# A fused attention and FFN kernel: its fallback flag, branch hints, last store, lane order, first loads and masks are changed

## The chip, the core and the metric

The kernel runs on one core of one Trainium2 chip. The metric is the device time of one execution in microseconds. Five engines with queues of their own work side by side: TensorE (PE, with its weight loads shown as PEld), VectorE (DVE), ScalarE (ACT), GpSimd (POOL) and SyncE (SP), which issues nearly all DMAs here. Each engine runs its instructions in the order in which they were built and waits at semaphores for the others.

## The reference

```python
def _attn_ref(q, k, v, n_sink, window):            # (4, 8, 768, 64) each; 4 and 128
    scores = (1.0 / np.sqrt(D)) * np.matmul(q, k.transpose(0, 1, 3, 2))
    is_sink = pos[None, :] < int(n_sink)
    rel = pos[:, None] - pos[None, :]
    keep = is_sink | ((rel >= 0) & (rel < int(window)))
    scores = np.where(keep, scores, -1000000000.0)
    a = np.exp(scores - np.max(scores, axis=-1, keepdims=True))
    a = a / (np.sum(a, axis=-1, keepdims=True) + 1e-09)
    return np.matmul(a, v).astype(np.float32)

def _moe_ref(x, w_in, w_out):                      # (3072, 512), (512, 2048), (2048, 512)
    h = x @ w_in
    g = np.where(h >= 1, h, np.where(h <= -1, 0.0, (h + 1.0) ** 2 / 4.0))
    return (g @ w_out).astype(np.float32)

x = np.ascontiguousarray(_attn_ref(...).transpose(0, 2, 1, 3)).reshape(B * S, H * D)
```

## The kernel before

**Work and tiles.** Attention falls into 64 units: a batch, a head and half a sequence, which is three tiles of 128 queries. A unit's scores are three matmuls (260 columns: two blocks of 128 keys and 4 sink keys; the first tile of a sequence has 128), then DVE adds the mask and finds each row's peak, ACT takes the exponential, PE transposes the result, ACT copies it back and PE multiplies by the values. The first 16 units go as eight pairs of heads (`pair_scores`, L656; the exponential, L676; `early_transp`, L699, with its copies L705, L706 and L708 by ACT; `pair_r`, whose copy xn is L762; `pair_av`, L722), and the first four of these stand ahead of everything else in `first_pairs`. The other 48 are native units, whose scores are L444 and whose q_l, the low part of the queries, is made by POOL (L426).

The FFN goes by eight chunks of 384 rows of x. `split` makes x from xn in a high (ACT, L875) and a low part (DVE, L876), `stage1` multiplies by w_in (L835), and ACT and DVE make g (L842 to L847); `stage2` multiplies by w_out (L858), and ACT copies 128 rows of the output to SBUF (L869), from where SP stores them (L871). All FFN products are three matmuls of high and low parts. The weights come as 64-bit words in 16 blocks of 1 MB (`block`: one load by SP, L359; three DVE steps L361 to L365, a cast of the high part by ACT, L367, and the low part by DVE, L368).

**Masks.** m0, m1, m1n and m2 are added to the scores. DVE makes them at the start from iotas of POOL and from the two parameters (par_i, loaded by SP). That code, and memsets of the sink tiles behind them, lie ahead of the region in which the order is fixed by hand, and are ordered by the scheduler.

**Order.** `Plan` records every step with its engine, a guessed time, and what it reads and writes. `order` runs a list schedule over these guesses, and the steps are then issued in that order, which the region of `tc.manual_schedule()` keeps. PE has two lanes, A (attention) and B (FFN); `turn` picks between their heads, when both are ready, by the share of each lane's work that is done. The loads of SP are ordered by the due time of their readers, and one may go a set lead ahead of it.

**The end.** `checks` and `result` make a flag: whether the inputs were of the kind for which the fast path is right. The plan has them behind all chunks: DVE's checks, a PE transpose (L978), and three small DVE steps (L972 to L974) that write the tile other. Then every engine loads other (L1030) and branches (L1031) over a general computation of more than 10,000 instructions to the closing block (L1098).

## Time and profile before

| | us |
|---|---|
| median of 3 runs | 689.83 (688.82 to 690.71) |
| profiled execution | 689.68 |
| its span | 688.0 |
| TensorE's matmuls | 671.2 (98%) |
| DVE | 501.6 (73%) |
| ACT | 489.2 (71%) |
| POOL | 237.3 (34%) |

The span runs from the first to the last instruction of the profiled execution. TensorE is busy for nearly all of it, so what is to be read are the stretches in which it is not. TensorE's granted clock is 1.00, the upper of its two levels, in all stretches in which it has matmuls.

### The profile page before, as it was taken

To read this page: it belongs to the slowest core of one execution; us is meant where nothing else is said; L and a number is where in the kernel's file an instruction comes from. 1 tells how busy PE (TensorE), PEld (TensorE's weight loads), DVE (VectorE), ACT (ScalarE), POOL (GpSimd) and SP (SyncE) were. 2 spreads that over 40 slices of the span, in tenths; PEclk is the share of its full clock that TensorE was granted. 3 is DMA by queue.
4 is the path that set the end of the run, shared out by engine and by line. 5 is a ranking of instruction groups with operands and counts; after the bars stand their busy time and mean duration, and the time that the engine had idled before them with its cause. 6 is when DMAs were issued, how large, how long until landed. Compare 5 with 4: busy or idle time off the path is not lost.

```text
span 688.0 us, 11934 instructions
## 1 busy us (share of the span) xinstructions
PE 671.2 (98%) x3853; PEld 601.7 (87%) x3853; DVE 501.6 (73%) x1421; ACT 489.2 (71%) x1245; POOL 237.3 (34%) x421
## 2 busy tenths in 40 slices
PE   6899999999999999999999999999999999999995
PEld 5688888889999999999999999999999999999994
DVE  6998999787767688686786877787787776733221
ACT  6887877777668777887778777797777866544332
POOL 3000014444433445453543454354453444300000
PEclk9999999999999999999999999999999999999999
DMA  6946433231223433434434433434424221000001
GB/s 220 333 170 240 141 143 117 60 92 49 61 65 117 126 110 126 142 98 145 128 93 147 123 105 128 135 118 134 124 89 123 67 89 43 1 31 16 1 0 51
DMA packets 41086, 73.94 MB, mean 107 GB/s; under 512 B 4344, under 2 KB 25656, under 8 KB 41016
## 3 DMA queue, kind: packets, MB, share of 16 engines
q1 hardware_dynamic: 41016, 73.09, 33.4%
q8 instruction: 33, 0.54, 0.3%
q14 instruction: 37, 0.30, 0.1%
HBM read 66.78 MB, written 6.29 MB: 106 GB/s over the span
## 4 chain that ended last, share of the span: by engine, by line
PE 87%; DVE 7%; ACT 2%; DMA 1%; issue 1%; POOL 0%; SPq 0%; POOLq 0%; DVEq 0%
PE o_ps L858 36%; PE h_ps L835 36%; PE ps_a L587 5%; PE ps_a L444 5%; PE ps_a L525 2%; DMA w<-w_in 1%; PE ps_a L656 1%; DVE wi L368 1%; PE ps_a L722 1%; DVE gl L847 1%; DVE x L876 1%; DVE ends L363 1%; ACT p L452 1%; DVE ends L361 1%; DVE w L365 1%
## 5 line engine op out<-in xcount | busy, mean ns | idle before, releaser
L835 PE MATMUL h_ps<-x,wi 128*128 128x384 f32 x1536 | 311.8, 340 | 0.8 <-DVE x L876 0.6
L835 PEld LDWEIGHTS h_ps<-x,wi 128*128 128x128 f32 x1536 | 262.5, 188 | 10.4 <-issue 2.0
L858 PE MATMUL o_ps<-w,gh 128*128 128x512 f32 x768 | 243.4, 398 | 0.0
L858 PE MATMUL o_ps<-w,gl 128*128 128x512 f32 x384 | 151.0, 393 | 0.0
L858 PEld LDWEIGHTS o_ps<-w,gh 128*128 128x128 f32 x768 | 134.1, 188 | 15.8 <-issue 1.5
L844 DVE SCALAR_TENSOR_TENSOR g<-g,h_ps 128x384 f32<-128x384 f32 x128 | 70.4, 550 | 67.1 <-ACT g L843 66.3
L842 ACT ACTIVATE g<-h_ps,half 128x384 f32<-128x384 f32 x128 | 73.9, 577 | 54.1 <-PE h_ps L835 53.2
L847 DVE TENSOR_TENSOR gl<-g,gh 128x384 fp32r<-128x384 f32 x128 | 77.0, 602 | 29.4 <-ACT gh L846 28.8
L452 ACT ACTIVATE p<-p,peak 128x260 f32<-128x260 f32 (+1 forms) x144 | 71.6, 497 | 37.2 <-DVE peak L449 35.0
L846 ACT CAST gh<-g 128x384 fp32r<-128x384 f32 x128 | 65.3, 510 | 45.1 <-DVE g L844 43.9
L426 POOL TENSOR_TENSOR q_l<-r,q_h 128x384 fp32r<-128x384 f32 x48 | 50.6, 1053 | 116.9 <-ACT q_h L425 116.8
L858 PEld LDWEIGHTS o_ps<-w,gl 128*128 128x128 f32 x384 | 72.0, 188 | 16.9
L449 DVE CUSTOM_DVE_ANT_0 p<-ps_a,m 128x260 f32<-128x260 f32 (+1 forms) x144 | 57.7, 408 | 21.7 <-PE ps_a L444 21.4
L843 ACT ACTIVATE g<-g 128x384 f32<-128x384 f32 x128 | 67.2, 525 | 3.2
L471 DVE CUSTOM_DVE_ANT_0 p<-p,stat 128x128 f32<-128x128 f32 x128 | 60.1, 496 | 2.3
L546 POOL TENSOR_SCALAR_AFFINE_SELECT pt<-pt 128x384 fp32r<-128x384 f32 (+1 forms) x96 | 49.1, 514 | 23.7 <-ACT pt L534 12.6
L498 POOL TENSOR_TENSOR v_s<-r,v_s 128x256 fp32r<-128x256 f32 (+1 forms) x48 | 36.2, 754 | 60.1 <-ACT v_s L497 59.0
L551 POOL TENSOR_SCALAR_AFFINE_SELECT pt<-pt 128x384 fp32r<-128x384 f32 (+1 forms) x96 | 50.4, 545 | 0.2
L587 PEld LDWEIGHTS ps_a<-pt,v_s 128*128 128x128 f32 x304 | 42.5, 188 | 2.5 <-POOL v_s L498 0.2
L444 PE MATMUL ps_a<-k_s,q_l 128*128 128x260 f32 (+1 forms) x144 | 40.7, 283 | 1.3 <-POOL q_l L426 1.1
L587 PE MATMUL ps_a<-pt,v_s 128*128 128x256 f32 (+1 forms) x304 | 41.9, 275 | 0.0
L444 PE MATMUL ps_a<-k_s,q_h 128*128 128x260 f32 (+1 forms) x144 | 39.6, 275 | 0.0
(161 smaller groups left out, 851.6 us busy)
## 6 DMA issues: line engine op xcount, KB each, us to landing
r<-qk SPq DMA_DIRECT2D x48, 192.0 KB, 2.4
k_r<-qk SPq DMA_DIRECT2D x32, 262.0 KB, 2.8
w<-w_in SPq DMA_DIRECT2D x8, 1024.0 KB, 7.5
again<-w_in SPq DMA_DIRECT2D x16, 512.0 KB, 4.1
again<-w_out SPq DMA_DIRECT2D x16, 512.0 KB, 3.8
w<-w_out SPq DMA_DIRECT2D x6, 1024.0 KB, 8.5
out<-o SPq DMA_DIRECT2D x23, 256.0 KB, 2.4
r<-vx SPq DMA_DIRECT2D x32, 128.0 KB, 2.1
```

What stands on the lines that cost most here:

```text
L444: nc.tensor.matmul(ps()[:, lo:260], lhsT=q()[:, i * P:(i + 1) * P], rhs=k_s()[:, c0:c0 + 260 - lo], start=(j == 0), stop=(j == len(qs) - 1))
L449: op(DVE, 215 if lo else 350, lambda: nc.vector.tensor_tensor_reduce(out=p()[:, i, lo:260], in0=ps()[:, lo:260], in1=m, scale=-0.125, scal ...
L452: op(ACT, 400 if lo else 500, lambda: nc.scalar.activation(p()[:, i, lo:260], p()[:, i, lo:260], AF.Exp, bias=peak[:, n, i:i + 1], scale=-1.0,
L471: nc.vector.tensor_tensor_reduce(out=own, in0=own, in1=p()[:, k, 0:P], scale=r, scalar=0.0, op0=ALU.add, op1=ALU.add, accum_out=stat()[:, ...
L587: nc.tensor.matmul(z, lhsT=w, rhs=y, start=(n == 0), stop=(n == len(mms) - 1))
L835: nc.tensor.matmul(h_ps()[:, :T], lhsT=w_i[j][:, w, ct * P:(ct + 1) * P], rhs=x()[:, y, ct], start=(ct == 0 and n == 0), stop=(ct == NCT - ...
L842: op(ACT, 490, lambda: nc.scalar.activation(g(), h_ps()[:, :T], AF.Relu, bias=half, scale=0.5), r=[h_ps], w=[g])
L843: op(ACT, 440, lambda: nc.scalar.activation(g(), g(), AF.Square), w=[g])
L844: op(DVE, 470, lambda: nc.vector.scalar_tensor_tensor(g(), g(), 1.0, h_ps()[:, :T], op0=ALU.min, op1=ALU.max), r=[h_ps], w=[g])
L846: op(ACT, 420, lambda: nc.scalar.copy(gh(), g()), r=[g], w=[gh])
L847: op(DVE, 500, lambda: nc.vector.tensor_tensor(gl(), g(), gh().bitcast(F32), op=ALU.subtract), r=[g, gh], w=[gl])
L858: nc.tensor.matmul(ps(), lhsT=gg()[:, tt * P:(tt + 1) * P], rhs=w_o[j][:, w], start=(j == 0 and n == 0), stop=(j == NJ - 1 and n == 2))
```

## The change

Seven parts, in the order of the program:

- **Hints.** `mark_branch_hint_location` names the branch "other", likely taken, for all engines; the `If` bears that label and a preferred fall-through block. In the built program one BRANCH_PREFETCH_HINT is the first instruction of the main block on each engine.
- **Masks.** The region with the fixed order begins ahead of the masks. They are made directly as terms to be added, in 13 small DVE steps in place of some 26; parts of m1 and m2, which are needed later, are plan steps of DVE, ACT and POOL, and the tables of the native units are made by a POOL step, `setup`.
- **First queries.** The first pair's q_h goes by ACT's DMA queue, not SP's.
- **Third pair's loads.** They go to tiles of the rings q_l and k_r, and no longer wait for the first pair's tiles.
- **Slack and blocks.** `turn` takes the other lane's head when it has been ready for over 800 ns and the chosen one has not. The plan's link rate is 380 bytes per ns for the 1 MB blocks and 260 for other loads (before, 330 for all), and a block may always go 8000 ns ahead of its due time.
- **Flag.** `decide` (checks, transpose, result) stands in the middle of the last chunk.
- **Halves.** The last 128x512 of the output is copied as two halves: columns 0 to 255 by ACT and stored by ACT's queue, columns 256 to 511 by DVE and stored by SP.

```diff
@@ class Plan
+SLACK = 800
-                heapq.heappush(later[o.eng], (max(o.ready, o.due - (3000 if o.due < 25000 else 8000)) if o.eng == SP else o.ready, o.n, o))
+                heapq.heappush(later[o.eng], (max(o.ready, o.due - (8000 if o.due > 25000 or o.bytes == 1 << 20 else 3000)) if o.eng == SP else o.ready, o.n, o))
...
-                return a if done[ka] * LEAD * total[kb] <= done[kb] * total[ka] else b
+                x, y = (a, b) if done[ka] * LEAD * total[kb] <= done[kb] * total[ka] else (b, a)
+                return y if x.ready + SLACK > t >= y.ready + SLACK else x
...
-                link = max(link, free[e]) + o.bytes / 330.0
+                link = max(link, free[e]) + o.bytes / (380.0 if o.bytes == 1 << 20 else 260.0)
@@ masks, ahead of the plan's steps
+    region = ExitStack()
+    region.enter_context(tc.manual_schedule())
...
-    nc.vector.tensor_scalar(m2, rel, w_f, None, op0=ALU.is_lt)
...
-    for m in (m0, m1, m1n, m2):
-        nc.vector.tensor_scalar(m, m, -1.0, -NEG, op0=ALU.add, op1=ALU.mult)
...
+    nc.vector.tensor_scalar(skn, kpos, n_f, NEG, op0=ALU.is_ge, op1=ALU.mult)
+    nc.vector.scalar_tensor_tensor(ahead, rel[:, KB:260], w_f, ahead, op0=ALU.is_ge, op1=ALU.max)
+    nc.vector.tensor_tensor(m0, ahead, skn, op=ALU.mult)
+    nc.vector.scalar_tensor_tensor(m1n[:, 0:P], rel[:, 0:P], w_f, skn, op0=ALU.is_ge, op1=ALU.mult)
+    nc.vector.tensor_scalar(m1n[:, KB:260], ahead, NEG, None, op0=ALU.mult)
@@ def pair_load(m)
-        q_h, k_h = qh_ring.new(), ks_ring.new()
+        q_h, k_h = (ql_ring.new(), kr_ring.new()) if m == 2 else (qh_ring.new(), ks_ring.new())
...
-        op(SP, 420, lambda: nc.sync.dma_start(q_h().bitcast(F32), qkp[b, h // 2, :, 0:T]), w=[q_h], size=P * T * 4)
+        if m:
+            op(SP, 420, lambda: nc.sync.dma_start(q_h().bitcast(F32), qkp[b, h // 2, :, 0:T]), w=[q_h], size=P * T * 4)
+        else:
+            op(ACT, 420, lambda: nc.scalar.dma_start(q_h().bitcast(F32), qkp[b, h // 2, :, 0:T]), w=[q_h])
@@ def first_pairs()
+        op(DVE, 3600, lambda: None, w=["masks"])
+        op(DVE, 200, lambda: nc.vector.tensor_scalar(m2[:, 0:P], rel[:, 0:P], w_f, NEG, op0=ALU.is_ge, op1=ALU.mult),
+           r=["masks"], w=["m2"])
+        op(ACT, 200, lambda: nc.scalar.copy(m2[:, P:KB], skn[:, 0:NSINK]), r=["masks"], w=["m2a"])
+        op(ACT, 300, lambda: nc.scalar.copy(m2[:, KB:260], m1n[:, KB:260]), r=["masks"], w=["m2a"])
+        op(ACT, 300, lambda: nc.scalar.copy(m1[:, P:260], m2[:, P:260]), r=["m2a"], w=["m1a"])
...
+        op(POOL, 9000, setup, r=["m1"], w=["setup"])
...
@@ def stage1, last step
+        if plan.on and (row0, j) == (last, NJ - 3):
+            op(HOST, 1, lambda: tc.mark_branch_hint_location("other", "LikelyTaken", list(mybir.ALL_ENGINES)), r=[gl])
@@ def stage2, the last output
-            op(ACT, 500, lambda: nc.scalar.copy(at(), ps()), r=[ps] + [("xn", c, a) for c in range(NCT) for a in range(2)]
-               if end else [ps], w=[o])
-            op(SP, 420, lambda: nc.sync.dma_start(out[row0 + tt * P:row0 + (tt + 1) * P, :], at()), r=[o], size=1 << 18)
...
+            op(ACT, 320, lambda: nc.scalar.copy(o[:, h0], ps()[:, h0]), r=[ps] + x_k, w=["end0"])
+            op(DVE, 320, lambda: nc.vector.tensor_copy(o[:, h1], ps()[:, h1]), r=[ps] + x_k, w=["end1"])
+            op(ACT, 420, lambda: nc.scalar.dma_start(rows[:, h0], o[:, h0]), r=["end0"])
+            op(SP, 420, lambda: nc.sync.dma_start(rows[:, h1], o[:, h1]), r=["end1"], size=1 << 17)
@@ the chunks
         if c == len(chunks) - 1:
             ffn, attn = ffn + tail, []
+            ffn.insert(len(ffn) // 2, ("A", 0.1, decide))
...
-    plan.group = "A", len(chunks) + 1, 0.1
...
-    with tc.If(other_v > 0):
+    with tc.If(other_v > 0, preferred_fallthrough_block=True, label="other"):
```

What this makes of the order, at three places. Line numbers of the changed kernel are some lines off: L670 there is L676 before (the exponential), L702, L699 and L700 are L708, L705 and L706 (the copies of the transposed tiles), L756 is L762 (xn), L842 is L835 and L650 is L656.

ACT among the first four pairs, from the first 128-column exponential of the third pair, before (p and pt are halves of the exponentials' tiles of a pair, ps_a the PSUM bank in which PE left the transposes):

```order
L676 ACTIVATE p_203,stat_310<-p_203,peak_97 128x128
L762 COPY xn_163<-ps_a_298 128x384
L676 ACTIVATE p_203,stat_310<-p_203,peak_97 128x260 x2
L676 ACTIVATE p_205,stat_310<-p_205,peak_97 128x260
L708 COPY pt_240<-ps_a_327 128x384
L705 COPY pt_240<-ps_a_335 128x256
L706 COPY v_s_177<-ps_a_335 4x128
L708 COPY pt_229<-ps_a_342 128x384
```

The same place on ACT now:

```order
L670 ACTIVATE p_175,stat_328<-p_175,peak_83 128x128
L702 COPY pt_216<-ps_a_318 128x384
L699 COPY pt_216<-ps_a_323 128x256
L700 COPY v_s_144<-ps_a_323 4x128
L702 COPY pt_206<-ps_a_332 128x384
L699 COPY pt_206<-ps_a_339 128x256
L700 COPY v_s_145<-ps_a_339 4x128
L670 ACTIVATE p_175,stat_328<-p_175,peak_83 128x260 x2
L670 ACTIVATE p_179,stat_328<-p_179,peak_83 128x260
```

The six copies moved ahead of the three exponentials of 260 columns.

PE at the end of the first four pairs, from the transposes of the fourth pair's first unit, before (wi is the first w_in block):

```order
L699 MATMUL ps_a<-ident,pt 128x128 x5
L701 MATMUL ps_a<-ident,pt 4x128
L835 MATMUL h_ps<-x,wi_155 128x384 x3
L699 MATMUL ps_a<-ident,pt 128x128 x5
L701 MATMUL ps_a<-ident,pt 4x128
L742 MATMUL ps_a<-ident,stat 64x128 x6
L835 MATMUL h_ps<-x,wi_155 128x384 x3
L722 MATMUL ps_a<-pt,vq_176 64x128 x2
```

And now:

```order
L693 MATMUL ps_a<-ident,pt 128x128 x5
L695 MATMUL ps_a<-ident,pt 4x128
L693 MATMUL ps_a<-ident,pt 128x128 x5
L695 MATMUL ps_a<-ident,pt 4x128
L736 MATMUL ps_a<-ident,stat 64x128 x6
L716 MATMUL ps_a<-pt,vq_143 64x128 x2
L716 MATMUL ps_a<-pt,vq_143 64x256 x4
L716 MATMUL ps_a<-v_s,vq_143 64x128 x2
L650 MATMUL ps_a<-k_s,q_h 128x128 x2
L650 MATMUL ps_a<-k_s,q_h 128x260 x2
L842 MATMUL h_ps<-x,wi_124 128x384 x15
```

The two pieces of three FFN matmuls stand no longer among the pairs, but behind them and the next pair's scores.

ACT from the last outputs to the branch, with the semaphores that each row waits for, before (xn is the tile that the last output is put into):

```order
L869 COPY o<-o_ps 128x512 [waits DMAHW4_49,PE_49]
L869 COPY o<-o_ps 128x512 [waits DMAHW5_49,PE_49]
L869 COPY xn<-o_ps 128x512 [waits PE_49]
L1030 TENSOR_LOAD other [waits DVE_49]
L1031 COMPARE_AND_BRANCH
```

And now:

```order
L876 COPY o<-o_ps 128x512 [waits DMAHW4_49,PE_49]
L876 COPY o<-o_ps 128x512 [waits DMAHW5_49,PE_49]
L882 COPY xn<-o_ps 128x256 [waits DVE_49]
L884 DMA out<-xn 128x256 [waits Activation_49]
L1042 TENSOR_LOAD other [waits DVE_49]
L1043 COMPARE_AND_BRANCH
```

The last copy is half as wide and waits for DVE, whose copy of the other half stands ahead of it, and a store by ACT stands ahead of the load of the flag.

## Rows read from the trace of the kernel before

**Rows 1.** Busy time by stretch; columns as in the line above them.

```profile
core 0: us, PE busy (x) PEld busy (x) DVE busy (x) ACT busy (x) POOL busy (x), PEclk, DMA share, GB/s
4.86:34.34 29.48, 26.57 (x227) 19.09 (x227) 25.97 (x87) 24.38 (x83) 4.86 (x23) 1.00 0.86 299
...
112.70:190.00 77.30, 75.31 (x426) 68.17 (x426) 61.12 (x186) 57.33 (x158) 36.50 (x67) 1.00 0.23 63
190.00:681.03 491.03, 491.03 (x2741) 449.90 (x2739) 337.23 (x982) 346.31 (x857) 188.56 (x316) 1.00 0.30 92
681.03:688.00 6.97, 0.00 (x0) 0.00 (x0) 0.56 (x3) 0.51 (x1) 0.00 (x0) 0.76 0.35 125
```

**Rows 2.** Waits of PE: what waited for what; us in total, times, longest.

```profile
PE ps_a L699 <- ACT pt L708: 1.4, 2, 0.7
...
PE ps_a L699 <- ACT xn L762: 0.6, 2, 0.3
```

**Rows 3.** Timeline of the start: start, duration, engine, line, what; idle time before.

```profile
1.24 0.42 SPq L616 DMA_DIRECT2D k_s<-qkp  x1
...
1.71 0.42 SPq L618 DMA_DIRECT2D q_h<-qkp  x1
...
4.86 1.20 PE L656 MATMUL o_ps<-k_s,q_h 64*128 64x128 f32 x5 [4.86 <-DMA q_h<-qkp]
...
7.71 0.28 DVE L277 TENSOR_SCALAR m<-m 128x260 f32<-128x260 f32 x1
```

**Rows 4.** Chain of waits, the first weight block: start, duration, what.

```profile
10.32 7.08 DMA w<-w_in
```

**Rows 5.** Timeline of the pairs, and one row from behind them.

```profile
16.55 0.45 ACT L708 COPY pt<-ps_a 128x384 f32<-128x384 f32 x1
...
17.05 0.44 PE L699 MATMUL ps_a<-ident,pt 128*128 128x128 f32 x2 [0.71 <-ACT pt L708]
...
20.19 1.15 ACT L367 CAST wi<-w 128x1024 fp32r<-128x1024 f32 x1 [0.69 <-DVE w L365]
...
34.34 0.96 PE L835 MATMUL h_ps<-x,wi 128*128 128x384 f32 x4 [0.61 <-DVE x L876]
...
128.09 0.33 PE L444 MATMUL ps_a<-k_s,q_l 128*128 128x128 f32 x1 [0.63 <-POOL q_l L426]
```

**Rows 6.** Timeline of the end.

```profile
680.53 0.39 PE L858 MATMUL o_ps<-w,gl 128*128 128x512 f32 x1
...
680.76 0.27 PE L978 MATMUL ps_a<-ident,flag 128*1 128x128 f32 x1
680.96 0.59 ACT L869 COPY xn<-o_ps 128x512 f32<-128x512 f32 x1
...
681.57 0.33 SPq L871 DMA_DIRECT2D out<-xn  x1
```

**Rows 7.** Durations by line (ns: least, median, most), and issue to landing.

```profile
L592 DVE TENSOR_TENSOR xn<-ps_a,xn x48: 539/556/562, 129.0 to 600.7; 64x384 f32<-64x384 f32 x48
...
L705 ACT COPY pt<-ps_a x16: 351/368/383, 10.3 to 96.1; 128x256 f32<-128x256 f32 x16
...
out<-xn SPq DMA_DIRECT2D x1, 256.0 KB, 2.0
```

**Rows 8.** Line L1031, the branch: ns, then first and last start in us.

```profile
L1031 SPq EVENT_SEMAPHORE  x8: 17/17/17, 686.0 to 686.6; - x8
L1031 ACTq COMPARE_BRANCH  x1: 50/50/50, 682.5 to 682.5; - x1
L1031 POOLq COMPARE_BRANCH  x1: 45/45/45, 682.6 to 682.6; - x1
...
L1031 PEldq COMPARE_BRANCH  x1: 4306/4306/4306, 682.6 to 682.6; - x1
L1031 POOLq EVENT_SEMAPHORE  x1: 17/17/17, 682.8 to 682.8; - x1
...
L1031 ACTq EVENT_SEMAPHORE  x1: 17/17/17, 685.5 to 685.5; - x1
```

More of the change, by code (lines that the diff above doesn't have):

```diff
@@ L913, in attn_ffn, with checks, decide, result @@
     spn = [t().bitcast(F32).rearrange("p t a d -> p (t a d)")[:, 0:P] for t in sinks0]
-    for t in spn:
-        nc.vector.memset(t, 0.0)
     ends = dec.tile([P, 2, DM], I32, name="ends")
     spare = dec.tile([P, 2, 2 * DM], I32, name="spare")
-    with tc.issue_after(behind):
-        nc.gpsimd.memset(ends, 0)
     p0 = [p_ring.new() for _ in range(2)]
     pt0 = [pt_ring.new() for _ in range(2)]
+    flag = const.tile([P, CT], F32, name="flag")
+    other = const.tile([1, 1], I32, name="other")
+    def checks():
+        v, both = nc.vector, chk[1]
+        pk = peak.rearrange("p u i -> p (u i)")
+        v.tensor_tensor(pk, pk, pk, op=ALU.mult)
+        v.tensor_reduce(flag[:, 1:2], pk, axis=mybir.AxisListType.X, op=ALU.add)
+        v.tensor_scalar(flag[:, 0:1], flag[:, 1:2], LARGE2, None, op0=ALU.is_lt)
+        for value, bound, o in ((n_f, float(NSINK), ALU.is_le), (w_f, float(P), ALU.is_le), (w_f, 1.0, ALU.is_ge)):
+            v.scalar_tensor_tensor(flag[:, 0:1], value, bound, flag[:, 0:1], op0=o, op1=ALU.mult)
+        v.tensor_scalar(both, both, 0x38383838, None, op0=ALU.bitwise_and)
+        v.tensor_scalar(both, both, 0x38383838, None, op0=ALU.bitwise_xor)
+        v.tensor_scalar(both.bitcast(F32), both, 0.0, None, op0=ALU.is_equal)
+        v.tensor_reduce(flag[:, 1:2], both.bitcast(F32), axis=mybir.AxisListType.X, op=ALU.min)
+        v.tensor_tensor(flag[:, 0:1], flag[:, 0:1], flag[:, 1:2], op=ALU.mult)
+    def decide():
+        ps = bank_a.new()
+        def result():
+            nc.vector.tensor_reduce(flag[0:1, 1:2], ps()[0:1, :P], axis=mybir.AxisListType.X, op=ALU.min)
+            nc.vector.tensor_scalar(flag[0:1, 2:3], flag[0:1, 1:2], -1.0, 1.0, op0=ALU.mult, op1=ALU.add)
+            nc.vector.tensor_copy(other, flag[0:1, 2:3])
+        op(DVE, 4000, checks, w=["flag", "both"] + [("peak", n, i) for n in range(len(units)) for i in range(CT)])
+        op(PE, 110, lambda: nc.tensor.transpose(ps()[0:1, :P], flag[:, 0:1], ident), r=["flag"], w=[ps])
+        op(DVE, 700, result, r=[ps], w=["flag"])
     def run(steps, c):
```

120 lines of the change are left out of this document (48 added, 72 removed).

## The prediction

> **What bounds the kernel now.** I read the busy times by stretch first, then what TensorE waits for, then the timelines of the places where it stands still. TensorE's matmuls fill all of the 491.03 us from 190 us to the last matmul, 26.57 of the 29.48 us from the first matmul to 34.34 us, and 75.31 of the 77.30 us from 112.7 to 190 us [rows 1]. So TensorE is idle for 4.86 us before its first matmul, for 2.91 us in the stretch of the first four pairs, for 1.99 us after 112.7 us and for 6.97 us behind its last matmul, some 16.7 us in all. The change adds no matmul and takes none away: the most that it can give is this idle time, and the most that it can lose is new idle time. The profiled execution took 689.68 us against a span of 687.96 us (1.7 us lie around the span); the median of the runs is 689.83 us. Each term below is a difference of spans, so I take the sum from the median. About 0.3%, or 2.1 us, is what a measurement of this kernel can tell from no change; 687.8 us is the border to faster, 691.9 us that to slower.
>
> In the pairs stretch two waits are for the copy pt of L708, of up to 0.7 us each, and two for the copy xn of L762, 0.6 us together; both copies are ScalarE's [rows 2].
>
> **The change, part by part. First queries and masks.** SP issues its second load, k_s, at 1.24 us and its third, q_h, at 1.71 us; the first matmul needs both and starts at 4.86 us [rows 3]. In the changed kernel q_h is ScalarE's first instruction, but k_s is still SP's second. So only the 0.47 us by which q_h was later can go, and a part of it goes again because two loads now share the link: -0.4 us, between 0 and -0.6 (the 0.47 and what the fewer loads ahead of k_s might save). DVE's last mask step ends at 7.99 us, between the first reductions of the scores [rows 3]. Half of these steps are gone, so the first reductions and exponentials come sooner; I count nothing for that here, because TensorE does not wait for them until the pairs stretch, where it is a part of that term. If the new steps were slower than the old ones, the first transposes would be late by it.
>
> **The third pair's loads and the blocks.** The first weight block was issued at 10.32 us and landed 7.08 us later [rows 4], because it stood behind two loads whose buffers TensorE still read. With the third pair's loads in buffers of their own and the longer lead, it is SP's eighth load, and no load ahead of it waits. Seven issues of some 0.43 us put its issue near 4 us [rows 3], and the same 7.08 us its landing near 11 us. Alone this gives nothing: no matmul uses the block before the end of the pairs. It lets DVE, which waited for it, decode earlier, and that is a part of the next term.
>
> **The pairs stretch.** At 16.55 us ScalarE starts the copy L708, right behind three exponentials of the next pair, and TensorE starts the transposes behind it 0.50 us later, at 17.05, after 0.71 us of idle time [rows 5]. In the changed order the exponentials of 260 columns stand behind the copies, so the copy comes about 1 us sooner (two of about 0.5 us), more than the 0.71. The second wait for pt has a cast of a weight slice ahead of it on ScalarE, of 1.15 us, at 20.19 us [rows 5]. In the changed order the first such cast stands behind all exponentials of the fourth pair, and this second 0.71 us has no cause left either. Against these 1.42 us: the pieces of the first FFN product that filled TensorE among the fourth pair's transposes now all stand behind the pairs. That is no loss of work, but ScalarE has no less to do, and the idle time can come back at the first FFN pieces. Before, these waited 0.61 us for an x piece ahead of 34.34 us [rows 5]; with one weight cast fewer ahead of the last x cast I take 0.4 us of that. The waits for xn stay. Together -1.8 us, between 0 (each wait moves to ScalarE's next copy) and -2.9 (all idle time of the stretch). Beyond zero it could grow by one weight cast, 1.15 us, if TensorE comes to the FFN pieces that much ahead of x.
>
> **Slack.** After 112.7 us TensorE loses 1.99 us, of which 0.63 us in one wait for GpSimd's q_l [rows 1, 5]. The rule that takes a lane's head which has been ready for 800 ns over one that is only just ready changes the order there. The trace shows no such choice. I take -0.3 us, half of that one wait, between -2.0 (all of it) and +1.3 (two more such waits). Nothing is to be had from 190 us on, where TensorE has no idle time.
>
> **Flag, halves and hints: the tail.** The last matmul ends at 680.92 us, ScalarE's copy of 512 columns takes 0.59 us from 680.96, SP issues the store at 681.57 [rows 6], and it lands 2.0 us later [rows 7], near 683.6. That is not what ends the span. All engines take the branch over the general case near 682.6 us. SP's next instruction starts at 686.0 us and ScalarE's at 685.5; TensorE's branch itself lasts 4.31 us, to 686.9 [rows 8]. GpSimd, which takes the same branch, goes on within 0.2 us. From SP's 686.0 to the end of the span, at 688.0, are another 1.9 us of semaphores. So 3 to 4.3 us pass in which no engine does anything but get to the code behind the branch.
>
> With the flag made inside the last chunk its transpose costs TensorE 0.11 us inside the stream (before, it ended at 681.03 us, 0.11 us behind the last matmul [rows 6]). If the hint works, each engine's branch costs GpSimd's 0.2 us, and the stores set the end. DVE copies one half of 256 columns: 0.42 us, halfway between its 0.28 us for 260 columns in SBUF [rows 3] and its 0.556 us for 384 columns from PSUM [rows 7]. ScalarE's half takes the 0.368 us of its other copies of 256 columns [rows 7]. They do not run side by side: in the built order ScalarE's copy waits for DVE's. With 0.03 us at each of two hand-overs ScalarE's store is issued at 681.81 us, 0.24 us later than SP's was, and lands near 683.85. SP's wait for it and 1.83 of the 1.9 us of semaphores end at 685.68 in place of 687.96, 2.28 us sooner; less the 0.11 us of the transpose the term is about -2.15 us. Engines that load the flag first (0.8 us) and branch are all there before 683.85.
>
> If the hint does nothing, the branches only start sooner: ScalarE's near 683.0 us, since it now issues a store ahead of it, with its next instruction 3.0 us later at 686.0; TensorE's near 681.8, so that its 4.31 us end at 686.1 in place of 686.9. The end is then 0.9 us sooner.
>
> **The sum** with a hint that works: -0.4 - 1.8 - 0.3 - 2.15 = -4.65 us, and 689.83 - 4.65 = 685.2 us.
>
> **Rival A: the hint changes nothing.** For it: in the built order the hint is the first instruction of each engine's main block, some 680 us ahead of the branch, and whatever is fetched on it has the whole kernel in which to be displaced. Against it: a hint that names a branch could be kept until the engine comes to it. No row of before shows a hint, so both prices of the branch, 0.2 us and 3.0 to 4.31, stand as ends. 689.83 - 0.4 - 1.8 - 0.3 - 0.9 = 686.4 us.
>
> The Trainium skill's page "Runtime: NRT & Kernel Launch", section "Instruction fetch mechanics", speaks for this rival. It says that instructions are fetched ahead strictly in order, and that a taken branch to a place outside the window has to wait for a transfer of it. The trace agrees as far as a plain branch goes, by the 3 to 4.31 us on four engines [rows 8]; by that rule, which knows no hint, the sum would be this rival's. No run here shows yet what a hint does.
>
> **Rival B: the pairs stretch keeps its idle time.** ScalarE is busy for 24.38 of the 29.48 us there [rows 1], and what is taken from one of its copies may wait at the next. Against it: the two longest waits have named causes that are gone. 689.83 - 0.4 - 0.3 - 2.15 = 687.0 us, and with rival A 688.2.
>
> **Rival C: slower, by a hint that fetches at the wrong time.** The hint stands where the main block begins. If it makes an engine fetch the far code in place of what comes next, the engine pays the price of a fetch there and then. It is not hidden: SP's loads and TensorE's first matmul come behind it. TensorE's price is the longest, 4.31 us [rows 8]. One such stall, with the tail of rival A, gives 686.4 + 4.31 = 690.7 us, no change that can be measured; two, the second where displaced code is wanted again, give 695.0 us. So it decides from the second stall on. Against it: all that stands between is in order, which is how the engines ran 680 us without one.
>
> **How the numbers follow.** The forecast, 0.53, has its own range from 683.4 to 686.1. Rival A has 0.22, rival B 0.16 (687.0 to 688.2), rival C 0.06, and 0.03 are for a growth of the pairs stretch or of the one after 112.7 us. The forecast, rival A and two thirds of B lie below 687.8: faster 0.85. The rest of B and of the growth, with one stall of C: same 0.10. Slower 0.05. The range goes from 683.0 us (all idle time of the pairs, 0.6 us at the head and 1.2 of the 1.99 us, in the forecast's sum) to 688.1, where B meets A.
>
> **What would show it.** Right: behind the branch each engine goes on within 0.3 us, and the last store's landing is what SP waits for; no wait for pt above 0.3 us before the first FFN product; a first matmul at 4.4 to 4.5 us. Wrong: branches that still take 3 to 4 us (A); waits for pt, xn or x of together over 2 us in the pairs stretch (B); first loads that are microseconds later than now (C). A TensorE idle time of over 1 us between 190 us and the last matmul would break the sum wholly.

## The result

The changed kernel takes 694.31 us (median; 693.82 to 695.40), the kernel before 689.92 us beside it (688.82 to 690.71): a ratio of 1.0067, with a 95% interval of 1.0054 to 1.0081. It is slower, where 685.2 us and faster were forecast. The profiled span is 693.4 us against 687.96.

The end is shorter and the start is shorter; the loss lies where TensorE had no idle time at all. The busy time of the engines by stretch in the changed kernel (columns as in [rows 1]):

```profile
4.05:31.96 27.91, 26.25 (x226) 19.63 (x226) 24.67 (x84) 24.68 (x86) 4.69 (x23) 1.00 0.84 301
...
190.00:400.00 210.00, 207.08 (x1167) 188.21 (x1166) 160.19 (x473) 158.06 (x405) 91.69 (x157) 1.00 0.38 114
400.00:600.00 200.00, 197.10 (x1111) 178.93 (x1110) 154.29 (x450) 146.70 (x372) 92.37 (x149) 1.00 0.33 101
...
687.91:693.40 5.49, 0.00 (x0) 0.00 (x0) 0.42 (x1) 0.37 (x1) 0.00 (x0) 0.97 0.42 148
```

In [rows 1] the stretch from 190 us on was full. Here 5.8 us are idle in it (210 - 207.08 and 200 - 197.10). The stretch behind the last matmul is 5.49 us, where it was 6.97. What TensorE waits for in the changed kernel (us in total, times, longest), beside [rows 2]:

```profile
PE o_ps L650 <- DMA k_s<-qkp: 4.1, 1, 4.1
PE ps_a L516 <- DVE peak L440: 3.6, 8, 0.8
PE ps_a L578 <- POOL v_s L489: 1.8, 4, 0.8
PE ps_a L435 <- POOL q_l L417: 1.7, 4, 0.8
PE ps_a L693 <- ACT pt L702: 1.4, 1, 1.4
```

The first matmul starts 0.8 us sooner. The two waits for pt have become one of 1.4 us, and the waits for xn are gone. The native units now have 16 waits, where they had three: the transposes (L516) wait for DVE's peak, the values (L578) for GpSimd's v_s, the scores (L435) for GpSimd's q_l. Idle time tells only a part, for the same 3853 matmuls are busy for 674.7 us in place of 671.2. In a dense row a matmul starts before the one ahead of it has ended (0.11 us behind its start, of a run of 0.28, in the rows below), and a delay shows as idle time only as far as it is longer than this overlap. At the 23 places with idle time in the changed kernel the next matmul starts 12.4 us later, all told, than the same pair of shapes does in a dense row, of which 9.1 us are idle. So a wait takes, by this estimate, some 0.14 us more than its idle time shows. The waits that were added explain some 1.5 of the 3.5 us in this way; by the same estimate most of the rest are delays too short to leave a gap.

One such place, on TensorE, in the changed kernel:

```profile
365.43 0.28 PE L435 MATMUL ps_a<-k_s,q_h 128*128 128x260 f32 x1
365.54 0.29 PE L435 MATMUL ps_a<-k_s,q_l 128*128 128x260 f32 x1
...
365.91 0.28 PE L435 MATMUL ps_a<-k_s,q_h 128*128 128x260 f32 x1
366.03 0.28 PE L435 MATMUL ps_a<-k_s,q_l 128*128 128x260 f32 x1
366.15 1.21 PE L842 MATMUL h_ps<-x,wi 128*128 128x384 f32 x6
368.14 0.55 PE L516 MATMUL ps_a<-ident,p 128*128 128x128 f32 x3 [0.79 <-DVE peak L440]
```

and what GpSimd, DVE and ScalarE did for it:

```profile
364.22 1.02 POOL L417 TENSOR_TENSOR q_l<-r,q_h 128x384 fp32r<-128x384 f32 x1 [1.98 <-ACT q_h L416]
...
366.87 0.54 DVE L851 SCALAR_TENSOR_TENSOR g<-g,h_ps 128x384 f32<-128x384 f32 x1
367.33 0.41 DVE L380 TENSOR_TENSOR both<-both,top 128x256 int32<-128x256 int32 x1
367.67 0.41 DVE L440 CUSTOM_DVE_ANT_0 p<-ps_a,m 128x260 f32<-128x260 f32 x1
...
368.59 0.51 ACT L443 ACTIVATE p<-p,peak 128x260 f32<-128x260 f32 x1
```

The unit's three score tiles stand on end (a tile of q_h and q_l each from 365.43 to 366.03), q_l had been finished at 365.24, 0.30 us ahead of its first reader, and DVE reaches the tiles' peaks only at 367.67, behind its own queue. Score tiles that the next tile follows at once are 85 of 144 in the built order, where it was 2 before.

The transposes at 368.14 do not wait for their own operand. They belong to the unit before, for the exponentials of the tiles scored here begin only at 368.59. They wait for a place to write to: all of the native units' steps on TensorE share a ring of three PSUM banks.

```python
    bank_a = ring(ps_a, 3, "ps_a", [P, 512], F32)
```

The unit's three score tiles fill the ring, and its first bank is free again when DVE's peak step has read it, at 368.08 us (367.67 + 0.41). All eight of these waits are of this kind: the transposes of one unit begin 63 to 65 ns behind the end of the peak step on the first score tile of the next.

### The profile page after: what moved, and what is told of

The parts are those of the page before. It is cut to its first block, busy times and chain, and to the rows that moved or that the text cites. A ratio compares the mean times of both kernels' runs of the same rounds, so it can differ in the third digit from the quotient of the medians.

```text
span 693.4 us, 11948 instructions
## 1 busy us (share of the span) xinstructions
PE 674.7 (97%) x3853; PEld 602.1 (87%) x3853; DVE 506.2 (73%) x1410; ACT 488.4 (70%) x1248; POOL 240.2 (35%) x425
## 4 chain that ended last, share of the span: by engine, by line
PE 58%; DVE 17%; ACT 10%; issue 7%; POOL 5%; DMA 2%; SPq 0%; POOLq 0%; ACTq 0%; DVEq 0%
PE h_ps L842 24%; PE o_ps L867 24%; DVE p L462 3%; ACT p L443 3%; PE ps_a L578 3%; PE ps_a L435 2%; DVE gl L854 2%; DVE g L851 2%; POOL pt L537 1%; DVE x L890 1%; POOL q_l L417 1%; PE ps_a L516 1%; DVE k_s L414 1%; DMA r<-qk 1%; ACT gh L853 1%
## 5 line engine op out<-in xcount | busy, mean ns | idle before, releaser
L842 PE MATMUL h_ps<-x,wi 128*128 128x384 f32 x1536 | 309.4, 340 | 0.2 <-DVE x L890 0.2
L842 PEld LDWEIGHTS h_ps<-x,wi 128*128 128x128 f32 x1536 | 264.0, 188 | 11.2 <-issue 2.9
L867 PEld LDWEIGHTS o_ps<-w,gh 128*128 128x128 f32 x768 | 139.7, 188 | 18.8 <-issue 0.5
L854 DVE TENSOR_TENSOR gl<-g,gh 128x384 fp32r<-128x384 f32 x128 | 79.1, 618 | 32.6 <-ACT gh L853 31.5
L417 POOL TENSOR_TENSOR q_l<-r,q_h 128x384 fp32r<-128x384 f32 x48 | 52.6, 1096 | 73.5 <-ACT q_h L416 73.1
L440 DVE CUSTOM_DVE_ANT_0 p<-ps_a,m 128x260 f32<-128x260 f32 (+1 forms) x144 | 53.0, 408 | 11.0 <-PE ps_a L435 10.7
L489 POOL TENSOR_TENSOR v_s<-r,v_s 128x256 fp32r<-128x256 f32 (+1 forms) x48 | 34.0, 708 | 40.1 <-ACT v_s L488 36.2
L578 PEld LDWEIGHTS ps_a<-pt,v_s 128*128 128x128 f32 x304 | 41.7, 188 | 5.3 <-POOL v_s L489 3.9
L578 PE MATMUL ps_a<-pt,v_s 128*128 128x256 f32 (+1 forms) x304 | 42.6, 277 | 2.0 <-POOL v_s L489 1.8
L435 PE MATMUL ps_a<-k_s,q_l 128*128 128x260 f32 (+1 forms) x144 | 38.3, 288 | 1.8 <-POOL q_l L417 1.7
L526 DVE TENSOR_TENSOR pt<-ps_a,pt 128x384 fp32r<-128x384 f32 x48 | 26.6, 553 | 18.0 <-ACT pt L525 12.3
```

The lines of the kernel that those rows point to most:

```text
L417: op(POOL, 1020, lambda: nc.gpsimd.tensor_tensor(q_l(), q_r(), q_h().bitcast(F32), op=ALU.subtract), r=[q_r, q_h], w=[q_l])
L578: nc.tensor.matmul(z, lhsT=w, rhs=y, start=(n == 0), stop=(n == len(mms) - 1))
L842: nc.tensor.matmul(h_ps()[:, :T], lhsT=w_i[j][:, w, ct * P:(ct + 1) * P], rhs=x()[:, y, ct], start=(ct == 0 and n == 0), stop=(ct == NCT - ...
L854: op(DVE, 500, lambda: nc.vector.tensor_tensor(gl(), g(), gh().bitcast(F32), op=ALU.subtract), r=[g, gh], w=[gl])
L867: nc.tensor.matmul(ps(), lhsT=gg()[:, tt * P:(tt + 1) * P], rhs=w_o[j][:, w], start=(j == 0 and n == 0), stop=(j == NJ - 1 and n == 2))
```

## The experiments: which number of the plan

The parts of the change other than the plan's three numbers (slack rule, link rates, lead of the blocks) stay in the first three of these.

**no_slack**

```diff
-                return y if x.ready + SLACK > t >= y.ready + SLACK else x
+                return x
```

> The changed kernel with the slack rule taken out of the choice between the two lanes; the new link rates and block lead stay. Theory: the slack rule makes the order in which TensorE waits from 190 us on (2.92 us idle from 190 to 400 us and 2.90 us from 400 to 600 us, where before there was none). Then that idle time goes, and with it the 3.5 us by which the matmuls' busy time grew: near 686 us. Rival, the new link rates make the order: idle time of over 4 us stays between 190 and 600 us and the time stays within 1.5 us of 694.3.

692.45 us. Half of the theory holds at most: 0.34 us idle are left from 190 to 400 us, but 3.42 us from 400 to 600. The slack rule is not the only cause.

**old_rates**

```diff
-                link = max(link, free[e]) + o.bytes / (380.0 if o.bytes == 1 << 20 else 260.0)
+                link = max(link, free[e]) + o.bytes / 330.0
```

> The changed kernel with the plan's link rate back at 330 bytes per ns for all loads; slack rule and block lead stay. Theory slack: time stays near 694 us, TensorE's idle time from 190 to 600 us stays at 4 us or more. Rival rates: near 686 us and no idle time there.

697.47 us, slower than the change itself, with 7.4 us of TensorE's idle time from 190 to 600 us. The rival falls as well: with the slack rule in, the old rates do not mend the order.

**old_plan** has both edits and the old lead:

```diff
-... o.due - (8000 if o.due > 25000 or o.bytes == 1 << 20 else 3000) ...
+... o.due - (3000 if o.due < 25000 else 8000) ...
```

> The changed kernel with slack rule, link rates and block lead all as before; flag, hints, halves, masks, first queries and third pair's loads stay. TensorE's order is then that of before but for some 67 rows. If the order is the whole loss: no idle time of TensorE from 190 us to the last matmul, and 689.9 less the tail's 1.5 us and the start's 1 to 2.5 us, 686 to 687.5 us. If something else of the change (the hint at the program's start, the flag inside the last chunk, GpSimd's setup) costs the middle: 692 us or more.

681.46 us, a ratio of 0.9882 to the kernel before. The plan's numbers are the whole loss, 12.85 us, and what they hid is a gain of 8.6 us (690.04 beside it), nearly twice the 4.65 us that were forecast for everything together. TensorE's waits behind the first matmul are three:

```profile
PE ps_a L516 <- DVE p L460: 0.4, 1, 0.4
PE ps_a L693 <- ACT pt L702: 0.4, 1, 0.4
PE ps_a L716 <- ACT pt L702: 0.2, 1, 0.2
```

The place of the timeline above now reads so on TensorE: between the score tiles stand six matmuls of the FFN each.

```profile
366.64 0.28 PE L435 MATMUL ps_a<-k_s,q_h 128*128 128x260 f32 x1
366.76 0.28 PE L435 MATMUL ps_a<-k_s,q_l 128*128 128x260 f32 x1
366.88 1.20 PE L842 MATMUL h_ps<-x,wi 128*128 128x384 f32 x6
367.92 0.28 PE L435 MATMUL ps_a<-k_s,q_h 128*128 128x260 f32 x1
```

**lead_only** (no slack rule, old rates, the new lead of the blocks):

> The changed kernel without the slack rule and with the old link rate; only the longer lead of the weight blocks stays of the plan's numbers. Score tiles on end: 1 of 144, as with the old plan. Theory: that count decides, so 681 to 683 us, idle time of TensorE only where the blocks are decoded, ahead of 115 us. Rival: the lead of the blocks makes a part of the loss by itself: 685 us or more.

685.28 us: the rival. The lead alone costs 3.8 us. 3.25 us are idle between the first and the last matmul, where old_plan has 1.03, most of it between 112 and 190 us. The largest wait, on TensorE:

```profile
115.49 1.20 PE L842 MATMUL h_ps<-x,wi 128*128 128x384 f32 x6
118.25 0.55 PE L516 MATMUL ps_a<-ident,p 128*128 128x128 f32 x3 [1.56 <-DVE peak L440]
```

There DVE came to the peak at 117.91 us, behind work that stood ahead of it in its queue: attention's own steps and parts of x, none of them the decoding of a block. It is the same wait for a bank, 64 ns behind the end of that peak step. By which way the earlier blocks bring this about was not shown.

**rates_only** (no slack rule, old lead, the new rates):

> The changed kernel with the new link rates alone of the plan's three numbers (no slack rule, old block lead). Score tiles on end: 57. With the new lead as well it was 692.45 us, and the new lead alone cost 3.8 us over 681.46. If rates and lead add up: 688.6 us, with idle time of TensorE between 400 and 600 us as with both. If the rates are the whole of it: 692.5. If the rates do no harm without the lead: 681.5 to 682.5.

695.36 us, more than with the lead as well (692.45). The three numbers do not add up; each picks another order.

**before_slack** is the kernel before with the slack rule alone:

> The kernel before with the slack rule alone added to the choice between the lanes. In its built order 66 of the 144 score tiles of the native units are followed at once by the next score tile, where it was 2 before and 85 in the changed kernel (58 without slack, 55 with the old rates, 1 with the old plan). Theory: score tiles on end make TensorE wait for DVE's peaks and GpSimd's q_l, at 0.13 to 0.3 us for each by the four runs: 699 to 709 us, idle time of over 5 us from 190 to 600 us. Rival: the order hurts only with the new head of the program: under 692 us.

697.14 us, 7.5 us slower than before, a little under the range, with 3.4 us of idle time from 190 to 600 us where over 5 were expected. The rule harms without any of the rest.

**slack_4000** is old_plan with the rule at 4000 ns:

```diff
-SLACK = 800
+SLACK = 4000
```

> The changed kernel with the plan's old link rate and block lead (681.46 us without any slack rule) and the slack rule at 4000 ns in place of 800. Score tiles on end in its built order: 22 of 144, between 1 with the old plan and 55 with 800 ns and the old rate (697.47 us, with the new lead in). Theory, the loss grows with that count, 0.13 to 0.3 us for each: 684 to 688 us. Rival, any use of the slack rule costs what 800 ns costs, or a few tiles on end cost nothing: 690 us or more, or 682 or less.

683.30 us: 1.8 us slower, with two waits for DVE's peak behind 400 us, of 0.5 us together. Its 22 score tiles on end cost under 0.1 us each, and in the profile 0.66 us of its loss is a first load that landed later (first matmul at 4.76 us in place of 4.10). So the count tells that an order is harmful, not by how much.

## The experiments: what such an order costs TensorE

**tiles_apart** keeps all new numbers and adds one rule:

```diff
+                if apart(a):
+                    return b
                 return y if x.ready + SLACK > t >= y.ready + SLACK else x
```

Here `apart(a)` says that TensorE's last step and attention's next are both score tiles.

> The changed kernel with all its new numbers (slack 800 ns, new rates, new lead) and one rule more in the choice between the lanes: when TensorE's last step was a score tile of a native unit, attention's next is one too, and the FFN lane's head is ready, the FFN takes its turn. Score tiles on end: 0 of 144, where it is 85 in the changed kernel (694.31 us). If score tiles on end are what TensorE pays for: 685 to 687 us, which is the 681.46 of the old plan with the 3.8 us of the lead, and no wait for DVE's peak between 190 and 600 us. If they are only a sign of an order that is bad in other ways too (transposes, values and q_l close behind each other): 690 us or more, and waits for q_l and v_s stay.

695.73 us. My theory fell, and what was written down against it came true. Its waits:

```profile
PE ps_a L584 <- POOL v_s L495: 3.6, 7, 1.0
PE ps_a L441 <- POOL q_l L423: 3.4, 5, 1.8
...
PE ps_a L522 <- DVE peak L446: 1.1, 4, 0.4
```

Those for DVE's peak are down from 3.6 to 1.1 us, those for GpSimd up from 3.5 to 7.0. So the next question was how long q_l was ready ahead of its reader. From the trace I took, for each of the 48 native units, the time from the end of GpSimd's q_l to the first matmul that reads it. The medians: 5.1 us before, 5.7 with old_plan, 5.2 with slack_4000; 1.9 with before_slack, 0.5 with no_slack, 0.4 in the changed kernel and with rates_only, 0.7 with tiles_apart. This number does not rank the orders either: old_rates, the slowest, has 2.5 us, and lead_only 4.9.

**pool_margin** keeps all new numbers, and in the plan's schedule a result of GpSimd counts 2 us later for attention's TensorE steps:

```diff
-                a.ready = max(a.ready, free[e] if a.eng == e and e != SP else end)
+                late = 2000 if e == POOL and a.eng == PE and a.group[0] == "A" else 0
+                a.ready = max(a.ready, free[e] if a.eng == e and e != SP else end + late)
```

> The changed kernel with all its new numbers, and in the plan's schedule a result of GpSimd counts 2 us later for the attention steps of TensorE. In the changed kernel's trace q_l was ready 0.40 us (median of 48 units) ahead of the first score that reads it, in the one with the old plan 5.7 us. Score tiles on end stay at 80 of 144. If operands that are ready too late are what TensorE pays for at GpSimd: the waits for q_l and v_s (3.5 us in the changed kernel, 7.0 us with the tiles apart) go below 0.5 us, those for DVE's peak (3.6 us) stay, and the time is 688 to 691 us. If the order is bad in yet another way: 693 us or more.

695.38 us. The first half came true: no wait for GpSimd is left (q_l is now ready 2.5 us ahead). The second did not: the waits for DVE's peak grew to 10.0 us, more than the 7.1 us that all three kinds had been in the changed kernel.

```profile
PE ps_a L517 <- DVE peak L441: 10.0, 16, 1.3
```

**apart_margin** has both edits:

> Both at once: score tiles apart (0 of 144 on end) and GpSimd's results counted 2 us later, with all of the changed kernel's numbers. Apart alone took the waits for DVE's peak from 3.6 to 1.1 us and let those for GpSimd grow from 3.5 to 7.0. If the two are the whole of the loss: waits for DVE's peak, q_l and v_s together under 2 us, and 685 to 688 us, 3.8 us of it the lead of the blocks above the 681.46 of the old plan. If there is a third cause: 690 us or more.

690.26 us, above the range and in that of a third cause: 4.05 us of the loss are gone, 8.8 us against old_plan are left. The 3.8 us that the lead alone cost are not a part of it that can be taken off. The last 2700 matmuls, those from some 195 us on, take 490.4 us here and 483.2 in old_plan, 7.2 us longer; in lead_only they take 1.9 us longer. Its waits:

```profile
PE ps_a L523 <- DVE peak L447: 2.8, 5, 1.2
PE h_ps L849 <- DVE x L897: 1.9, 3, 1.5
```

None is for GpSimd, and those for the FFN's x have grown from one of 0.2 us. What these runs show is this: in the old order TensorE comes to an attention step when what the step needs has been there for microseconds, and in the new ones when it is only just there. For q_l this is the median above, 5.7 us against 0.4. For the bank of the transposes it is the time from the end of the peak step that frees it to their start: in the median 2.1 us before and with old_plan, 2.2 with slack_4000, 0.6 in the changed kernel, with no_slack, rates_only and pool_margin, 1.0 with tiles_apart, 0.5 with apart_margin. The transposes' own operand is not what is late: its last piece is ready 4.8 to 5.7 us ahead in every one of these orders. Take away one of the waits, and the next one comes up. Both rules together give back 4 of the 12.85 us. Why the plan, with other rates, comes to such an order was not tested, nor was a ring of more than three banks.

## The experiments: the start

**third_back** is old_plan with the third pair's loads in their old rings:

```diff
-        q_h, k_h = (ql_ring.new(), kr_ring.new()) if m == 2 else (qh_ring.new(), ks_ring.new())
+        q_h, k_h = qh_ring.new(), ks_ring.new()
```

> The changed kernel with the plan's old numbers, and the third pair's loads back in the rings where they wait for TensorE. Its score tiles on end are 2. The last matmul ended at 674.29 us with these loads early, at 680.92 us in the kernel before; 2.3 us of that are waits gone from the first four pairs. If the early loads made that gain: waits for pt and xn of 1 us and more ahead of 34 us, and 682.5 to 684 us. If the masks, done earlier and in fewer steps, made it: 681.5 to 682 us and TensorE's waits there unchanged.

686.35 us, 4.9 us slower, more than expected. The waits that come back lie in the pairs and behind them:

```profile
PE h_ps L842 <- DVE x L890: 0.8, 1, 0.8
PE ps_a L693 <- ACT pt L702: 0.8, 1, 0.8
PE ps_a L516 <- DVE peak L440: 0.7, 1, 0.7
PE ps_a L693 <- DVE xn L723: 0.6, 2, 0.3
```

**before_third** is the kernel before with the opposite edit alone:

> The kernel before with the third pair's loads alone put into the rings q_l and k_r. In the changed kernel with the old plan these loads were worth 4.9 us (686.35 against 681.46). If they are worth that without the new masks too: near 685 us, with no wait of TensorE for pt of 0.7 us ahead of 34 us and fewer behind 112 us. If they need the masks to be early: 688 us or more.

684.56 us, a ratio of 0.9915 to the kernel before (690.12 beside it): 5.6 us from one line, without the masks. Its waits for pt are 0.4 us in place of [rows 2]'s 1.4, and none is left for xn or q_l. What held these loads, and the block behind them, are SP's waits ahead of 11 us in the kernel before: for the first pair's scores ahead of the third pair's loads (issued at 7.43 us), and for the second pair's ahead of the fourth's (9.47 us). First SP's waits there, then the third pair's k_s in before_third:

```profile
SPq L616 <- PE ps_a L656: 4.3, 2, 3.2
```

```profile
3.12 0.43 SPq L616 DMA_DIRECT2D k_r<-qkp  x1
```

There the block is issued at 8.24 us, before at 10.32 [rows 4].

**first_back** is old_plan with the first q_h on SP's queue:

> The changed kernel with the plan's old numbers, and the first pair's q_h back on SP's queue. First matmul at 4.10 us with it on ScalarE's queue, at 4.86 in the kernel before. If the queue makes the whole of that: first matmul near 4.7 us or later, 682.0 to 682.3 us. If it is the 0.4 us of the forecast: 681.9. If the masks' order made it, not the queue: 681.5.

682.74 us, 1.3 us slower, above the range; first matmul at 4.90 us in place of 4.10. The wait's name differs: with ScalarE's queue it is k_s (4.1 us, as in the changed kernel), with SP's it is q_h:

```profile
PE o_ps L650 <- DMA q_h<-qkp: 4.9, 1, 4.9
```

0.8 us of it are the first matmul. The other 0.5 us are no more than what profiles of one order differ by: idle time is the same (1.1 and 1.0 us), and TensorE's busy time is 669.2 us in old_plan and 670.0 in old_plan_whole, which differ only at the end.

The masks were not tested apart. The third pair's loads (5.6 us alone), the queue (1.3) and the shorter end (1.7) make up the 8.6 us of old_plan, so little is left for them, if the parts add.

## The experiments: the tail

The last output and the branch (L1043) in the changed kernel:

```profile
687.95 0.42 DVE L883 COPY xn<-o_ps 128x256 f32<-128x256 f32 x1 [3.29 <-PE o_ps L867]
688.40 0.33 SPq L885 DMA_DIRECT2D out<-xn  x1
688.40 0.37 ACT L882 COPY xn<-o_ps 128x256 f32<-128x256 f32 x1 [0.55 <-DVE xn L883]
688.81 0.37 ACTq L884 DMA_DIRECT2D out<-xn  x1
```

```profile
L1043 SPq EVENT_SEMAPHORE  x8: 17/17/17, 690.4 to 692.0; - x8
...
L1043 PEldq COMPARE_BRANCH  x1: 497/497/497, 685.3 to 685.3; - x1
...
L1043 ACTq COMPARE_BRANCH  x1: 68/68/68, 689.9 to 689.9; - x1
L1043 ACTq EVENT_SEMAPHORE  x1: 17/17/17, 690.4 to 690.4; - x1
```

```profile
out<-xn SPq DMA_DIRECT2D x1, 128.0 KB, 1.9
out<-xn ACTq DMA_DIRECT2D x1, 128.0 KB, 2.7
```

TensorE's branch takes 0.50 us in place of 4.31 [rows 8], ScalarE goes on 0.5 us behind its own in place of 3.0. The longest of SP's waits ends with the landing of ScalarE's half, 2.7 us behind its issue at 688.81, and the span ends 1.85 us behind that landing.

**old_plan_no_hint** takes the hint out of old_plan:

```diff
-        if plan.on and (row0, j) == (last, NJ - 3):
-            op(HOST, 1, lambda: tc.mark_branch_hint_location("other", "LikelyTaken", list(mybir.ALL_ENGINES)), r=[gl])
```

> The changed kernel with the plan's old numbers and without the hint instruction; the If keeps its label and its fall-through block. If the hint is what makes the branch short: TensorE's branch takes 3 to 4.3 us again and ScalarE resumes 3 us behind its branch, near 5.0 us behind the last matmul; the end is 0.7 to 1.6 us later, 682.2 to 683.1 us. If the block's layout does it and not the hint: 681.5 us, and branches as short as with it. If the branches are long but hidden since the flag is early: 681.5 to 682.

682.35 us (681.43 to 683.01; old_plan 681.19 to 681.78). The branches are long again:

```profile
L1041 PEldq COMPARE_BRANCH  x1: 3676/3676/3676, 672.4 to 672.4; - x1
...
L1041 ACTq COMPARE_BRANCH  x1: 54/54/54, 677.0 to 677.0; - x1
...
L1041 ACTq EVENT_SEMAPHORE  x1: 17/17/17, 680.0 to 680.0; - x1
```

It is the hint that makes them short, and it is worth about 0.9 us. The runs overlap, but the stretch behind the last matmul is 6.18 us in the profile, against 5.31 in old_plan and 5.1 to 5.5 in all kernels with hint, early flag and halves. TensorE's long branch is hidden, since with the early flag it is taken at 672.4 us, while matmuls still run. Nor do the other long branches set the end: SP is through at 678.8 us, ahead of the landing of ScalarE's half. That comes 4.34 us behind the last matmul in place of 3.47, and the span ends 1.84 us behind it in both kernels. So here the 0.9 us are a later landing.

**whole** puts one copy and one store in place of the halves:

```diff
-            op(ACT, 320, lambda: nc.scalar.copy(o[:, h0], ps()[:, h0]), r=[ps] + x_k, w=["end0"])
-            op(DVE, 320, lambda: nc.vector.tensor_copy(o[:, h1], ps()[:, h1]), r=[ps] + x_k, w=["end1"])
-            op(ACT, 420, lambda: nc.scalar.dma_start(rows[:, h0], o[:, h0]), r=["end0"])
-            op(SP, 420, lambda: nc.sync.dma_start(rows[:, h1], o[:, h1]), r=["end1"], size=1 << 17)
+            op(ACT, 500, lambda: nc.scalar.copy(o[:, :DM], ps()), r=[ps] + x_k, w=["end0"])
+            op(SP, 420, lambda: nc.sync.dma_start(rows, o[:, :DM]), r=["end0"], size=1 << 18)
```

> The changed kernel with one copy of 512 columns by ScalarE and one store by SP at the end, as before, in place of the two halves. From the rows of the changed kernel: the last matmul ends at 687.91, ScalarE's half lands at 691.51, 3.6 us behind it; before, the whole landed 2.69 us behind it. If the halves cost this, the end comes 0.9 us sooner, 693.4 us. If the halves cost only the 0.24 us of the forecast, 694.1. If SP's waits do not hang on the landing at all, 694.3.

693.76 us, 0.55 us less. On old_plan the same edit, **old_plan_whole**:

> The changed kernel with the plan's old numbers (681.46 us) and, at the end, one copy and one store in place of the halves. On the changed kernel that was worth 0.55 us of the median, and 0.55 us from the last matmul to the end. If the tail is its own: 680.9 us. If it is worth only the 0.24 us of the forecast: 681.2.

681.77 us, 0.3 us more than old_plan. The medians have two signs, but the profiles tell more. From the last matmul to the span's end the two kernels with the whole take 4.91 and 4.92 us, those with the halves 5.45 (693.36 - 687.91) and 5.31. So beside the early flag the halves cost some 0.4 to 0.5 us, and what hides it in old_plan_whole lies ahead of the last matmul (671.0 us from the first to the last, against 670.2).

**flag_end** is old_plan with `decide` behind all chunks, as the flag was before:

> The changed kernel with the plan's old numbers, and the flag made behind all chunks as before, with hint and halves kept. The flag is then ready some 0.8 us behind the last matmul, each engine loads it in up to 0.8 us and has a hinted branch of 0.5 us or less, so all are through about 2.5 us behind the last matmul, while the last half lands 3.5 us behind it. If the landing sets the end: 681.3 to 681.8 us, so the early flag is worth nothing beside the hint. If SP's or ScalarE's store now waits behind its load of the flag: 682.2 us or more.

680.99 us (680.22 to 681.28), a ratio of 0.9869: 0.5 us better than old_plan, and the stretch behind the last matmul is 4.63 us in place of 5.31. The early flag is not needed beside the hint, and costs a little. ScalarE's half now lands sooner:

```profile
out<-xn ACTq DMA_DIRECT2D x1, 128.0 KB, 1.9
```

The DMA packets of the traces tell where the landing may lose its time. In old_plan three packets of 8 KB with instructions run from 2.1 to 3.6 us behind the last matmul, among the packets of ScalarE's store (1.9 to 3.0 us). In flag_end they come at 3.1 us, behind the store's last (2.4 us), and in old_plan_no_hint there are six, and one of 16 KB at 2.1 us. That they delay the store fits these times, but no run shows it apart.

**flag_end_whole** has both of these edits:

> The changed kernel with the plan's old numbers, the flag behind all chunks (680.99 us with the halves) and one copy and one store at the end. The whole landed 2.3 us behind its issue with the early flag, the last half 1.9 us with the late one, but is issued 0.2 us sooner. If the last landing sets the end: 680.8 to 681.4 us, no difference that can be measured. If ScalarE's store was what the early flag disturbed and the whole is free of that: 680.5.

681.06 us, no difference. The fastest kernels of this study are these two and old_plan, 8.6 to 9.1 us below the kernel before beside them.

## Why the prediction was wrong

- **Slack.** The step that failed, with the two below: the plan's three numbers were put at -0.3 us together, and they cost 12.85 us (old_plan). The term was read from one wait after 112.7 us, and it said "Nothing is to be had from 190 us on". That is true: the last 2700 matmuls, those from some 195 us on, take 483.4 us before and 483.2 in old_plan. But it left out what is to be lost there: they take 493.7 us in the changed kernel. A rule in the choice between lanes acts on all of TensorE's order, and I had looked at its start and its end alone. before_slack gives its price without the rest: 7.5 us. In the change, taking it out alone gives back 1.9 us (no_slack), for the new rates do harm of the same kind by themselves. The bound of +1.3 was two waits of the size of the one that was there, though the two lanes' order from 190 us on was before me: 2 score tiles on end, and 85 in the change. The sign that the prediction itself named for a broken sum, over 1 us of idle time behind 190 us, is there with 5.8 us.
- **Link rates.** The prediction has no term for them. rates_only is 13.9 us above old_plan.
- **Blocks sooner.** The first block was issued at 4.18 us and landed at 11.47, as worked out. "Alone this gives nothing" should have asked what it takes: the lead costs 3.8 us by lead_only.
- **Third pair's loads.** Also put at nothing but a part of the pairs' -1.8 us; worth 5.6 us alone (before_third). The prediction had seen what they do: two waits for TensorE stood ahead of the first weight block. In before_third the stretch from 112 to 190 us is full too, so the waits there, which I had given to the slack rule, came with these loads; by which way was not followed.
- **Pairs stretch.** Forecast 1.8 of 2.9 us. In the changed kernel 1.66 us are idle in it (27.91 - 26.25), a gain of 1.25; with old_plan the two waits there are 0.6 us together. The first of the two causes named, the order of copies and exponentials, held. The second fell: the cast of a weight slice does stand behind the exponentials now, but it still stands ahead of the next copy for pt, and TensorE's one wait there is for that copy.

```profile
24.48 1.10 ACT L360 CAST wi<-w 128x1024 fp32r<-128x1024 f32 x1
25.48 0.46 ACT L702 COPY pt<-ps_a 128x384 f32<-128x384 f32 x1
```

```profile
26.00 0.76 PE L693 MATMUL ps_a<-ident,pt 128*128 128x128 f32 x5 [1.40 <-ACT pt L702]
```

- **First queries.** -0.4 forecast, -0.8 measured. The step "only the 0.47 us can go" took k_s's landing as fixed, and gave a part of the gain back to a shared link; k_s landed at 3.92 us in place of 4.22.
- **Tail.** -2.15 forecast, -1.48 measured (6.97 - 5.49). The hint made the branches short, though ScalarE and DVE go on 0.5 and 0.6 us behind theirs and not 0.2. ScalarE's half is issued 0.90 us behind the last matmul as worked out, and its landing sets the end, but it lands 2.7 us later, not 2.0. That term is 0.7 us off, and flag_end shows that the early flag is behind it.
- **Rivals.** A falls by the branches of 0.5 us and less; its tail, 0.9 us shorter without a working hint, is what old_plan_no_hint has (6.18 us from the last FFN matmul to the end, 7.04 before). Without the hint four engines go on 2.9 to 3.7 us behind the start of their branch in old_plan_no_hint, GpSimd 0.2. The Trainium skill's page "Runtime: NRT & Kernel Launch", section "Instruction fetch mechanics", says that a taken branch to a target outside the fetched window waits for a transfer of it. The four engines agree with that; with the hint, though it stands some 680 us ahead, no engine has a wait of that size. B does not hold either: 1.25 us of the pairs' idle time are gone, and the loss lies elsewhere. C gave nearly the measured time, 695.0 us, by a mechanism that is not there: SP's first load was issued at 0.89 us in place of 0.79 (0.79 again in old_plan_no_hint), so the hint costs about 0.1 us at the start. A time near the result showed nothing about the cause.
- **The bound.** The cases that the range was made of were all of the start and the end. Nothing in it stood for the 410 us between, in which most of the order had been rewritten.

## What to carry to other kernels

When a change touches the rule that sets an order, compare the whole order before pricing any place in it: how many rows moved, how many steps of one lane stand on end, how far each reader stands behind its maker, and how long a buffer has been free when its next writer comes. A stretch without idle time is the place where a new order can lose most. And undo a bundle part by part: one line of this one was worth 5.6 us, and three numbers beside it hid that.

## What the runs showed of the hardware that I had not expected

- A branch hint that is executed at 0.7 to 0.9 us, 46 to 51 ns on each engine, still makes the branch some 670 to 690 us later short: 0.5 us on TensorE in place of 3.7 to 4.3.
- The half of 128 KB on ScalarE's queue landed 2.4 to 2.8 us behind its issue with the hint and the early flag, 3.4 us without the hint, and 1.9 us with the late flag, as SP's half did in all runs. Engines take their branch while it is under way with the late flag too (676.4 to 676.7 us, landing at 677.30), so that alone is not it. What differs in the packets is when instructions are fetched, as told above.
- TensorE's branch of 3.7 us ran while its matmuls did, in old_plan_no_hint: its sequencer was at 672.4 us, the last matmul ended at 675.0.
